# Attention and a gated MLP on one core: the last batch's normalization split over three engines, its spatial blocks in a row, its last products by token tile

## The chip, the cores and the metric

The kernel runs on one core of a Trainium2 chip. The core has a matrix engine (TensorE, PE in the profile; its weight loads are listed apart as PEld), a vector engine (VectorE, DVE), an engine for functions of one argument (ScalarE, ACT), a general engine (GpSimd, POOL) and a sync engine (SP) that here only issues DMAs. Each engine works through its own queue in order; an instruction waits for semaphores that others raise. The engines share a working memory of 128 partitions (SBUF); matmul results go to a second memory (PSUM) in buffers of 512 fp32 columns or multiples, and POOL does not touch those.

The metric is the time of one execution on the device in microseconds (us); lower is better. The times shown are medians of several executions. The profile is of one execution, which has its own time.

## The reference

Two layers, each for 8 batches of 384 tokens:

```python
# attention: 16 query heads, 4 key/value heads, head size 64
scores = scale * np.matmul(q, k.transpose(0, 1, 3, 2))
attn = softmax(scores);  x = np.matmul(attn, v)          # x: (8, 384, 1024) once the heads are joined
# gated MLP with a spatial (token to token) product
h = np.maximum(x @ w_in, 0.0)                            # w_in: 1024 x 1024
u, v = h[..., :512], h[..., 512:]
v_n = (v - mu) / np.sqrt(var + 1e-06)                    # mean and variance over the 512 features
v_s = np.einsum('ts,bsd->btd', w_spatial, v_n) + b_spatial[None, :, None]
out = (u * v_s) @ w_out                                  # w_out: 512 x 1024, out: (8, 384, 1024) fp32
```

The output is fp32; the kernel's matmuls take fp16 and accumulate in fp32.

## The kernel before

The 384 tokens of a batch are three tiles of 128 (`NT = 3`). The 1024 inner features of x are eight blocks (`NB = 8`), the 512 features of u and of v four blocks (`NM = 4`).

The program's order is written out by hand. The main loop (L594 on) goes over 18 score steps per batch: two score matmuls, an exponential on ACT, then the weighting with v. Between these it takes work of the MLP from a generator, `stream()` (L424), so many matmul columns per step (`run_fill`). The MLP of a batch runs behind its own attention, under the attention of the next one. For batch 7, the last, there is no next one: what is left of its MLP when the main loop has ended is issued in one go (`for _ in fill`). Each engine gets its instructions in the order in which this generator and the loop issue them, and runs them in that order.

What `stream()` does for a batch:

- `v_tile(b, st)` (L288): v of one token tile, eight matmuls of 128x512 (L294); then on DVE a relu into SBUF (`vr`, L304) and the statistics (L306, L307).
- `u_block(b, m)` (L358): u of one feature block for all tokens, transposed, so features on partitions and 384 tokens as columns: eight matmuls of 128x384 (L361), then a relu on ACT into `uT` (L372). In block 0, after the fourth matmul, `normal(b)` is issued.
- `normal(b)` (L311): the reciprocal standard deviation on ACT (L314, L315), minus mean times that on DVE (`nmr`, L316), and for each of the three token tiles the normalized `vn` as one multiply-add on POOL (L322), 128x512 to fp16.
- `gate(b, m)` (L375): one spatial block. Three matmuls of 128x384 over the three tiles of `vn` (L380) into `psp`; DVE adds the bias (`g`, L390); then the product with `uT` into `gT` (L392). That product is on POOL, in the last batch on DVE for blocks 1 and 3.
- `project(b, tt, half)` (L395): the output of one token tile and one half of its columns: four matmuls over the blocks of `gT` (L406), a copy from PSUM to SBUF (L415; the first half on DVE, the second on ACT), and an output DMA from SP's queue. In the last batch each piece has its own DMA (L419), and the last half of the last tile is cut in two pieces of 256 columns.

In the last batch the order before is: v of tiles 1 and 2, u of blocks 0, 1 and 2, gates 0 and 1, u of block 3, gates 2 and 3, then the six projections. Tile 0 of v comes earlier, in front of the projections of batch 6.

PSUM buffers of `pv`, `pu`, `psp` and `po` come from one pool of three (`ps_ck`), handed out in the order of use: a matmul group that begins in a buffer waits for the reader of the group three places before it. The first spatial block takes over the buffer of u's block 0, so it waits for that block's relu. The scores have a pool of their own (`ps_sc`, two buffers).

Of the kernel before, what the change touches and what calls it, by code (L numbers as in the profile page):

```python
# [9 lines left out]
FP32 = mybir.dt.float32  # L10
FP16 = mybir.dt.float16
AF = mybir.ActivationFunctionType
ALU = mybir.AluOpType
# [4 lines left out]
def kernel(  # L18
# [16 lines left out]
    nc = tc.nc  # L35
    P = 128
    B, HQ, S, D = q.shape
# [4 lines left out]
    NT = S // P  # L42
    NB = DM // P
    NM = DH // P
    G = HQ // HKV
    assert (HQ, HKV, S, D, DM, DFF) == (16, 4, 384, 64, 1024, 1024)
    scale = D ** -0.5
# [8 lines left out]
    moe = ctx.enter_context(tc.tile_pool(name="moe", bufs=2))  # L56
    small = ctx.enter_context(tc.tile_pool(name="small", bufs=4))
    ops = ctx.enter_context(tc.tile_pool(name="ops", bufs=4))
    ps_sc = ctx.enter_context(tc.tile_pool(name="ps_sc", bufs=2, space=PSUM))
    ps_av = ctx.enter_context(tc.tile_pool(name="ps_av", bufs=1, space=PSUM))  # L60
    ps_ck = ctx.enter_context(tc.tile_pool(name="ps_ck", bufs=3, space=PSUM))
# [29 lines left out]
    def load_q0(j, lo, hi, eng):  # L91
# [9 lines left out]
    load_q0(0, 1, 3, nc.sync)  # L101
    load_q0(1, 1, 3, nc.sync)

    need = {AF.Exp, AF.Relu, AF.Copy, AF.Ln}
    set_id = next(
        i for i, (_, f) in enumerate(get_activation_tables(nc.m.arch).items()) if need <= f
    )
# [2 lines left out]
            name=nc.get_next_instruction_name(), act_func_set_id=set_id, ins=[], outs=[]  # L110
# [3 lines left out]
    w_in16 = cst.tile([P, NB, DFF], FP16, name="w_in16")  # L114
    w_out16 = cst.tile([P, NM, DM], FP16, name="w_out16")
    wsT16 = cst.tile([P, NT, S], FP16, name="wsT16")
# [27 lines left out]
    bias_b = cst.tile([P, S], FP32, name="bias_b")  # L144
# [121 lines left out]
    def x_tile(b):  # L266
        if b not in xts:
            xts[b] = att.tile([P, NT, NB, P], FP16, name=f"xt_{b}", tag="xt")
        return xts[b]
# [16 lines left out]
    mvs, v_rs, v_ns, uTs, gTs, osbs = {}, {}, {}, {}, {}, {}  # L286

    def v_tile(b, st):  # L288
        if st == 0:
            mvs[b] = small.tile([P, NT, 2], FP32, name=f"mv_{b}", tag="mv")  # L290
            v_rs[b] = []
        pv = ps_ck.tile([P, 512], FP32, name=f"pv_{b}_{st}", tag="ck")
        for kt in range(NB):
            nc.tensor.matmul(  # L294
                pv,
                x_tile(b)[:, st, kt],
                w_in16[:, kt, DH:DFF],
                start=(kt == 0),
                stop=(kt == NB - 1),
            )  # L300
            if kt < NB - 1:
                yield 512
        vr = moe.tile([P, DH], FP32, name=f"vr_{b}_{st}", tag="vr", bufs=4)
        nc.vector.tensor_scalar(vr, pv, 0.0, None, op0=ALU.max)  # L304
        stats = small.tile([P, 6], FP32, name=f"stats_{b}_{st}", tag="stats")
        nc.vector.bn_stats(stats, vr)  # L306
        nc.vector.bn_aggr(mvs[b][:, st, :], stats)  # L307
        v_rs[b].append(vr)
        yield 512

    def normal(b):  # L311
        rstd = small.tile([P, NT], FP32, name=f"rstd_{b}", tag="rstd")
        nmr = small.tile([P, NT], FP32, name=f"nmr_{b}", tag="nmr")
        nc.scalar.activation(rstd, mvs[b][:, :, 1], AF.Ln, bias=eps_t)  # L314
        nc.scalar.activation(rstd, rstd, AF.Exp, scale=-0.5)  # L315
        nc.vector.scalar_tensor_tensor(  # L316
            nmr, mvs[b][:, :, 0], -1.0, rstd, op0=ALU.mult, op1=ALU.mult
        )
        v_ns[b] = []
        for st in range(NT):  # L320
            vn = moe.tile([P, DH], FP16, name=f"vn_{b}_{st}", tag="vn", bufs=6)
            nc.gpsimd.tensor_scalar(  # L322
                vn,
                v_rs[b][st],
                rstd[:, st : st + 1],
                nmr[:, st : st + 1],
                op0=ALU.mult,
                op1=ALU.add,
            )
            v_ns[b].append(vn)  # L330

    def uT_tile(b):
        if b not in uTs:
            uTs[b] = moe.tile([P, NM, S], FP16, name=f"uT_{b}", tag="uT")
        return uTs[b]
# [22 lines left out]
    def u_block(b, m):  # L358
        pu = ps_ck.tile([P, 512], FP32, name=f"pu_{b}_{m}", tag="ck")
        for kt in range(NB):  # L360
            nc.tensor.matmul(  # L361
                pu[:, 0:S].rearrange("p (t s) -> p t s", t=NT),
                w_in16[:, kt, m * P : (m + 1) * P],
                x_tile(b)[:, :, kt],
                start=(kt == 0),
                stop=(kt == NB - 1),
            )
            if m == 0 and kt == 3:
                normal(b)
            if kt < NB - 1:  # L370
                yield S
        nc.scalar.activation(uT_tile(b)[:, m, :], pu[:, 0:S], AF.Relu)  # L372
        yield S

    def gate(b, m):  # L375
        if m == 0:
            gTs[b] = moe.tile([P, NM, S], FP16, name=f"gT_{b}", tag="gT")
        psp = ps_ck.tile([P, 512], FP32, name=f"psp_{b}_{m}", tag="ck")
        for st in range(NT):
            nc.tensor.matmul(  # L380
                psp[:, 0:S],
                v_ns[b][st][:, m * P : (m + 1) * P],
                wsT16[:, st, :],
                start=(st == 0),
                stop=(st == NT - 1),
            )
            if st < NT - 1:
                yield S
        g = moe.tile([P, S], FP32, name=f"g_{b}_{m}", tag="g", bufs=4)
        nc.vector.tensor_tensor(g, psp[:, 0:S], bias_b, ALU.add)  # L390
        by = nc.vector if b == B - 1 and m % 2 else nc.gpsimd
        by.tensor_tensor(gTs[b][:, m, :], g, uTs[b][:, m, :], ALU.mult)  # L392
        yield S

    def project(b, tt, half):  # L395
        last = b == B - 1
        rows = out[b].rearrange("(p t) d -> p t d", t=NT)
        if half == 0:
            osbs[b, tt] = ops.tile([P, DM], FP32, name=f"osb_{b}_{tt}", tag="osb")
        osb = osbs[b, tt]  # L400

        cuts = (512, 768, 1024) if last and tt == NT - 1 and half else (512 * half, 512 * half + 512)
        for i, (lo, hi) in enumerate(zip(cuts, cuts[1:])):
            po = ps_ck.tile([P, 512], FP32, name=f"po_{b}_{tt}_{half}_{i}", tag="ck")
            for m in range(NM):
                nc.tensor.matmul(  # L406
                    po[:, 0 : hi - lo],
                    gTs[b][:, m, tt * P : (tt + 1) * P],
                    w_out16[:, m, lo:hi],
                    start=(m == 0),  # L410
                    stop=(m == NM - 1),
                )
                if m < NM - 1:
                    yield hi - lo
            (nc.scalar.copy if half and not i else nc.vector.tensor_copy)(  # L415
                osb[:, lo:hi], po[:, 0 : hi - lo]
            )
            if last:
                nc.sync.dma_start(rows[:, tt, lo:hi], osb[:, lo:hi])  # L419
            elif half:  # L420
                nc.sync.dma_start(rows[:, tt, :], osb)
            yield hi - lo

    def stream():  # L424


        for b in range(B):
            last = b == B - 1
            if b == 0:
                yield from v_tile(0, 0)  # L430
                yield from v_tile(0, 1)
                yield from u_tile(0, 0)
                yield from v_tile(0, 2)
                yield from u_tile(0, 1)
                yield from u_tile(0, 2)
            else:
                yield from v_tile(b, 1)
                yield from v_tile(b, 2)
                for m in range(NM):
                    yield from u_block(b, m)  # L440
                    if last and m == 2:
                        yield from gate(b, 0)
                        yield from gate(b, 1)
            for m in range(2 if last else 0, NM):
                yield from gate(b, m)
            if not last:
                yield from v_tile(b + 1, 0)
            for tt in range(NT):
                for half in range(2):
                    yield from project(b, tt, half)  # L450
# [108 lines left out]
    for b in range(B):  # L559
# [16 lines left out]
        for m in range(6):  # L576
# [4 lines left out]
            elif m > 3:  # L581
                at(s0 + 3 * m + 5, x_turn, b, 2, 4 * (m - 4), 4 * (m - 3))

    fill = stream()
    owed = 0.0
    total = NU * B
# [7 lines left out]
    for n in range(total + 6):  # L594
# [7 lines left out]
        for hh in range(2):  # L602
            b, r = divmod(n - 3 - hh, NU)
# [42 lines left out]
```

## Time and profile before

| | |
|---|---|
| time, median of 3 runs | 253.52 us (253.1 to 254.39) |
| the profiled execution: its own time | 253.12 us |
| its span, first to last instruction | 251.3 us |
| PE busy | 240.9 us, 96% of the span, 2430 matmuls |
| ACT busy | 168.2 us, 67% |
| DVE busy | 139.7 us, 56% |
| POOL busy | 98.3 us, 39% |
| granted TensorE clock | 1.00 |
| HBM read and written | 25.95 MB and 12.58 MB |

The profile names an instruction group by its line, engine and operation, with the tiles it writes and reads (`psp<-wsT,vn`: psp written from wsT and vn), the shapes, how many there were and how long they took. "Idle before" is the time for which the engine had nothing to do ahead of such an instruction, and the arrow names what ended it. The chain of waits is followed back from the last instruction: at each step to what released it, or to the instruction ahead of it on the same engine. Matmuls are pipelined: the next starts before the one ahead has ended, so a stream of them is measured by the distance of their starts.

### The profile page before, as it was taken

How to read it: one execution, taken by the hardware profiler on the slowest of the kernel's cores; microseconds unless marked ns; L12 is line 12 of the kernel's file. 1: busy time of each engine (PE TensorE's matmuls, PEld its weight loads, DVE VectorE, ACT ScalarE, POOL GpSimd, SP SyncE). 2: the span in 40 equal slices, each digit the busy share in tenths (PEclk: the TensorE clock that was granted, in tenths of full speed). 3: DMA queues.
4: the chain of work that ended last, by engine and by line, in shares of the span. 5: the costliest groups of instructions: out<-in, count | busy, mean ns of one | idle time of the engine just before them, and what ended most of it. 6: DMA issues, size and time to landing. Idle time of an engine off the chain costs nothing.

```text
span 251.3 us, 6020 instructions
## 1 busy us (share of the span) xinstructions
PE 240.9 (96%) x2430; PEld 125.7 (50%) x2430; DVE 139.7 (56%) x368; ACT 168.2 (67%) x215; POOL 98.3 (39%) x142
## 2 busy tenths in 40 slices
PE   7898998999999999999999999999999999999883
PEld 7564657534455444544455445544455445544442
DVE  2455776854626755474626655474636655465462
ACT  3996566678696687768696687768696687741211
POOL 2698837871035701392036602391035003320320
PEclk9999999999999999999999999999999999999999
DMA  7999998999289964997399956997392452106006
GB/s 179 268 285 251 301 285 238 297 224 265 88 182 330 171 230 85 266 233 216 121 199 324 185 200 66 281 253 227 111 171 49 111 183 44 34 12 250 0 22 232
DMA packets 73981, 46.93 MB, mean 187 GB/s; under 512 B 48113, under 2 KB 68913, under 8 KB 73953
## 3 DMA queue, kind: packets, MB, share of 16 engines
q1 hardware_dynamic: 68832, 37.63, 59.4%
q0 software_dynamic: 4080, 8.65, 13.8%
q8 instruction: 19, 0.31, 0.5%
q10 hardware_dynamic: 1040, 0.26, 0.5%
q14 instruction: 10, 0.07, 0.1%
HBM read 25.95 MB, written 12.58 MB: 153 GB/s over the span
## 4 chain that ended last, share of the span: by engine, by line
PE 87%; DVE 7%; issue 1%; ACT 1%; POOL 1%; POOLq 0%; DVEq 0%
PE av L247 17%; PE pv L294 16%; PE sc L233 15%; PE po L406 15%; PE pu L361 13%; PE psp L380 6%; PE warm L504 3%; DVE stats L306 2%; DVE vr L304 2%; DVE x L259 2%; PE pu L344 1%; PE qps L200 1%; ACT aT L240 1%; POOL vn L322 1%; PE xps L275 1%
## 5 line engine op out<-in xcount | busy, mean ns | idle before, releaser
L240 ACT ACTIVATE aT<-sc 128x1024 f16<-128x1024 f32 x144 | 139.6, 1021 | 52.9 <-PE sc L233 52.7
L247 PEld LDWEIGHTS <-aT 128*128 128x128 f16 x1152 | 43.4, 97 | 32.9 <-DVE x L259 12.9
L322 POOL TENSOR_SCALAR vn<-vr,rstd,nmr 128x512 f16<-128x512 f32 x24 | 18.1, 767 | 99.6 <-DVE r L257 85.7
L247 PE MATMUL av<-v,aT 128*128 128x65 f16 x1152 | 52.3, 194 | 1.6 <-DVE x L259 1.2
L294 PE MATMUL pv<-w_in,xt 128*128 128x512 f16 x192 | 49.5, 378 | 0.0
L257 DVE RECIPROCAL r<-av 128x4 f32<-128x4 f32 x96 | 17.1, 178 | 58.3 <-PE av L247 57.8
L406 PE MATMUL po<-w_out,gT 128*128 128x512 f16 (+1 forms) x196 | 48.2, 375 | 0.9 <-POOL gT L392 0.9
L233 PE MATMUL sc<-qT,kT 64*128 64x512 f16 x288 | 45.0, 382 | 0.7 <-ACT aT L240 0.4
L259 DVE TENSOR_TENSOR x<-av,r 128x256 f16<-128x256 f32 x96 | 40.7, 424 | 3.4
L361 PE MATMUL pu<-xt,w_in 128*128 128x384 f16 x224 | 41.7, 326 | 0.0
L392 POOL TENSOR_TENSOR gT<-g,uT 128x384 f16<-128x384 f32 x30 | 26.5, 914 | 29.4 <-DVE g L390 29.4
L361 PEld LDWEIGHTS <-w_in 128*128 128x128 f16 x224 | 20.2, 97 | 14.7 <-issue 2.5
L406 PEld LDWEIGHTS <-gT 128*128 128x128 f16 x196 | 17.0, 97 | 19.4 <-issue 2.9
L170 POOL CAST q<-q 128x768 f16<-128x768 f32 (+1 forms) x36 | 24.9, 732 | 3.1 <-DMA q<-in_q_dram 3.1
L415 DVE COPY osb<-po 128x512 f32<-128x512 f32 (+1 forms) x25 | 16.8, 671 | 11.6 <-PE po L406 11.6
L294 PEld LDWEIGHTS <-xt 128*128 128x128 f16 x192 | 16.2, 97 | 13.5 <-issue 0.7
L415 ACT COPY osb<-po 128x512 f32<-128x512 f32 (+1 forms) x24 | 13.9, 580 | 12.4 <-PE po L406 12.3
L304 DVE TENSOR_SCALAR vr<-pv 128x512 f32<-128x512 f32 x24 | 16.5, 687 | 10.2 <-PE pv L294 10.0
L233 PEld LDWEIGHTS <-kT 64*128 64x128 f16 x288 | 8.9, 94 | 26.6 <-issue 24.4
L380 PE MATMUL psp<-wsT,vn 128*128 128x384 f16 x96 | 19.6, 326 | 0.6 <-POOL vn L322 0.6
L390 DVE TENSOR_TENSOR g<-psp,bias_b 128x384 f32<-128x384 f32 x32 | 16.4, 552 | 5.9 <-PE psp L380 5.9
L306 DVE BATCH_NORM_STATS2 stats<-vr 128x6 f32<-128x512 f32 x24 | 16.7, 695 | 0.8
(49 smaller groups left out, 125.8 us busy)
## 6 DMA issues: line engine op xcount, KB each, us to landing
out_dram<-osb SPq DMA_DIRECT2D x21, 512.0 KB, 2.9
q<-in_q_dram SPq DMA_DIRECT2D x10, 768.0 KB, 7.2
q<-in_q_dram POOLq DMA_DIRECT2D x4, 768.0 KB, 10.4
v<-in_v_dram SPq DMA_DIRECT2D x6, 384.0 KB, 8.7
w_in<-in_moe_w_in_dram POOLq DMA_DIRECT2D x4, 512.0 KB, 9.7
k<-in_k_dram SPq DMA_DIRECT2D x5, 384.0 KB, 4.2
out_dram<-osb SPq DMA_DIRECT2D x5, 256.0 KB, 2.0
q<-in_q_dram SPq DMA_DIRECT2D x2, 512.0 KB, 7.2
```

The costliest lines, as they stand in the source:

```text
L170: f(q16s[b, j][:, lo:hi, :, hh, :], src[:, hh, lo:hi])
L233: nc.tensor.matmul(sc[:, hh], kTs[b][half, j, t * P : (t + 1) * P], qTs[b, j][half, qt], start=True, stop=True,)
L240: nc.scalar.activation(aTs[b, m][:, t], sc, AF.Exp, scale=scale)
L247: nc.tensor.matmul(av[:, i, :], aTs[b, m][:, t, hh, i * P : (i + 1) * P], v1[b % 2][:, 2 * j + hh, t, 0 : D + 1], start=(t == 0), stop=(t ...
L259: nc.vector.tensor_tensor(x16s[b][:, qt, blk : blk + 2].rearrange("p k (i d) -> p (k i) d", i=2), av[:, :, 0:D], r.to_broadcast([P, G, D]) ...
L294: nc.tensor.matmul(pv, x_tile(b)[:, st, kt], w_in16[:, kt, DH:DFF], start=(kt == 0), stop=(kt == NB - 1),)
L306: nc.vector.bn_stats(stats, vr)
L361: nc.tensor.matmul(pu[:, 0:S].rearrange("p (t s) -> p t s", t=NT), w_in16[:, kt, m * P : (m + 1) * P], x_tile(b)[:, :, kt], start=(kt == 0 ...
L380: nc.tensor.matmul(psp[:, 0:S], v_ns[b][st][:, m * P : (m + 1) * P], wsT16[:, st, :], start=(st == 0), stop=(st == NT - 1),)
L392: by.tensor_tensor(gTs[b][:, m, :], g, uTs[b][:, m, :], ALU.mult)
L406: nc.tensor.matmul(po[:, 0 : hi - lo], gTs[b][:, m, tt * P : (tt + 1) * P], w_out16[:, m, lo:hi], start=(m == 0), stop=(m == NM - 1),)
L415: (nc.scalar.copy if half and not i else nc.vector.tensor_copy)(osb[:, lo:hi], po[:, 0 : hi - lo])
```

## The change

Three places, all of them for the last batch alone; the lines of the other batches are renumbered but the same.

1. `normal(b)`: of the three normalized tiles, tile 0 stays on POOL, tile 1 is computed on DVE and tile 2 on ACT, there as an activation with the function Identity, a scale and a bias per partition. Identity joins the list of functions from which the table set is chosen at the start.
2. `stream()`: u of blocks 0, 1 and 2, then a new function `last_gate()`. It runs the four spatial blocks one after another, then u of block 3 in two pieces: the first token tile (128 columns) and the other two (256 columns), in PSUM buffers of the scores' pool, each with its own relu on ACT. The products of blocks 0 and 1 are on POOL, over all tokens. Those of blocks 2 and 3 are cut as block 3 is: block 2's first token tile on POOL, the other three pieces on DVE.
3. `project()`: the last half of the last token tile is cut at 896 instead of 768, into 384 and 128 columns.

```diff
-    need = {AF.Exp, AF.Relu, AF.Copy, AF.Ln}
+    need = {AF.Exp, AF.Relu, AF.Copy, AF.Ln, AF.Identity}
...
-            nc.gpsimd.tensor_scalar(
-                vn,
-                v_rs[b][st],
-                rstd[:, st : st + 1],
-                nmr[:, st : st + 1],
-                op0=ALU.mult,
-                op1=ALU.add,
-            )
+            a, c = rstd[:, st : st + 1], nmr[:, st : st + 1]
+            if b == B - 1 and st == 2:
+                nc.scalar.activation(vn, v_rs[b][st], AF.Identity, scale=a, bias=c)
+            else:
+                by = nc.vector if b == B - 1 and st == 1 else nc.gpsimd
+                by.tensor_scalar(vn, v_rs[b][st], a, c, op0=ALU.mult, op1=ALU.add)
...
-        by = nc.vector if b == B - 1 and m % 2 else nc.gpsimd
-        by.tensor_tensor(gTs[b][:, m, :], g, uTs[b][:, m, :], ALU.mult)
+        nc.gpsimd.tensor_tensor(gTs[b][:, m, :], g, uTs[b][:, m, :], ALU.mult)
         yield S
+
+    def last_gate():
+        b = B - 1
+        gT = gTs[b] = moe.tile([P, NM, S], FP16, name=f"gT_{b}", tag="gT")
+        uT = uT_tile(b)
+        gs = []
+        for m in range(NM):
+            psp = ps_ck.tile([P, 512], FP32, name=f"psp_{b}_{m}", tag="ck")
+            for st in range(NT):
+                nc.tensor.matmul(
+                    psp[:, 0:S],
+                    v_ns[b][st][:, m * P : (m + 1) * P],
+                    wsT16[:, st, :],
+                    start=(st == 0),
+                    stop=(st == NT - 1),
+                )
+                yield S
+            g = moe.tile([P, S], FP32, name=f"g_{b}_{m}", tag="g", bufs=4)
+            nc.vector.tensor_tensor(g, psp[:, 0:S], bias_b, ALU.add)
+            gs.append(g)
+            if m < 2:
+                nc.gpsimd.tensor_tensor(gT[:, m], g, uT[:, m], ALU.mult)
+        first, rest = slice(0, P), slice(P, S)
+        m = NM - 1
+        for part in (first, rest):
+            pu = ps_sc.tile([P, 512], FP32, name=f"pu_{b}_{m}_{part.start}", tag="sc")
+            n = part.stop - part.start
+            for kt in range(NB):
+                nc.tensor.matmul(
+                    pu[:, 0:n].rearrange("p (t s) -> p t s", s=P),
+                    w_in16[:, kt, m * P : (m + 1) * P],
+                    x_tile(b)[:, part.start // P : part.stop // P, kt],
+                    start=(kt == 0),
+                    stop=(kt == NB - 1),
+                )
+                yield n
+            nc.scalar.activation(uT[:, m, part], pu[:, 0:n], AF.Relu)
+        for by, m, part in (
+            (nc.gpsimd, 2, first),
+            (nc.vector, 3, first),
+            (nc.vector, 2, rest),
+            (nc.vector, 3, rest),
+        ):
+            by.tensor_tensor(gT[:, m, part], gs[m][:, part], uT[:, m, part], ALU.mult)
...
-        cuts = (512, 768, 1024) if last and tt == NT - 1 and half else (512 * half, 512 * half + 512)
+        cuts = (512, 896, 1024) if last and tt == NT - 1 and half else (512 * half, 512 * half + 512)
...
-                for m in range(NM):
-                    yield from u_block(b, m)
-                    if last and m == 2:
-                        yield from gate(b, 0)
-                        yield from gate(b, 1)
-            for m in range(2 if last else 0, NM):
-                yield from gate(b, m)
+                for m in range(NM - last):
+                    yield from u_block(b, m)
+            if last:
+                yield from last_gate()
+            else:
+                for m in range(NM):
+                    yield from gate(b, m)
```

## The prediction

> **What bounds the kernel now.** I read the chain of waits on the page first, then the timeline of the last stretch on all engines, then the line of the gate product, then the output queue.
>
> ```profile
> PE 87%; DVE 7%; issue 1%; ACT 1%; POOL 1%; POOLq 0%; DVEq 0%
> ```
>
> TensorE (PE) sets 87% of the span. With one batch after another something always fills it, so what the other engines do counts only where PE has nothing else to run. That is the last batch: from 229.3 us on there is no attention work left, and the edit touches nothing before it. Timeline of the last batch (start, duration in us, engine, line, operation, count, idle before):
>
> ```profile
> 235.04 0.20 ACT L315 ACTIVATE rstd<-rstd 128x3 f32<-128x3 f32 x1
> 235.15 0.91 ACT L372 ACTIVATE uT<-pu 128x384 f16<-128x384 f32 x2
> 235.28 0.16 DVE L316 SCALAR_TENSOR_TENSOR nmr<-mv,rstd 128x3 f32<-128x3 f32 x1 [0.60 <-ACT rstd L315]
> 235.64 2.26 POOL L322 TENSOR_SCALAR vn<-vr,rstd,nmr 128x512 f16<-128x512 f32 x3 [13.84 <-PE pu L361]
> 236.67 0.33 PE L380 MATMUL psp<-wsT,vn 128*128 128x384 f16 x1
> 237.21 0.34 PE L380 MATMUL psp<-wsT,vn 128*128 128x384 f16 x1 [0.22 <-POOL vn L322]
> 237.96 0.82 PE L380 MATMUL psp<-wsT,vn 128*128 128x384 f16 x4 [0.41 <-POOL vn L322]
> ```
>
> The first spatial block needs the three normalized tiles in turn, and GpSimd (POOL) delivers them 0.75 us apart. PE takes a 128x384 matmul every 0.1625 us: four in 0.82 us are three steps and one matmul of 0.326. The third should have started at 236.67 + 2 x 0.1625 = 236.995 and started at 237.96: **0.97 us lost**. (The idle figures in brackets are smaller, because the modelled ends of matmuls reach into the gaps; starts are the safer measure.)
>
> ```profile
> 238.41 1.04 DVE L390 TENSOR_TENSOR g<-psp,bias_b 128x384 f32<-128x384 f32 x2 [2.97 <-PE psp L380]
> 238.62 1.46 PE L361 MATMUL pu<-xt,w_in 128*128 128x384 f16 x8
> 239.11 0.91 POOL L392 TENSOR_TENSOR gT<-g,uT 128x384 f16<-128x384 f32 x1 [1.21 <-DVE g L390]
> 239.56 0.89 DVE L392 TENSOR_TENSOR gT<-g,uT 128x384 f16<-128x384 f32 x1
> 240.68 1.04 DVE L390 TENSOR_TENSOR g<-psp,bias_b 128x384 f32<-128x384 f32 x2 [0.24 <-PE psp L380]
> 240.90 0.59 PE L406 MATMUL po<-w_out,gT 128*128 128x512 f16 x2
> 241.38 0.91 POOL L392 TENSOR_TENSOR gT<-g,uT 128x384 f16<-128x384 f32 x1 [1.36 <-DVE g L390]
> 241.83 0.88 DVE L392 TENSOR_TENSOR gT<-g,uT 128x384 f16<-128x384 f32 x1
> 242.35 5.13 PE L406 MATMUL po<-w_out,gT 128*128 128x512 f16 x26 [0.86 <-POOL gT L392]
> ```
>
> The first projection runs two matmuls, 0.216 us apart (0.59 - 0.379 for the second's own length), and then waits: the products of blocks 2 and 3 come after the last spatial block. The third should start at 240.90 + 0.43 = 241.33 and starts at 242.35, 1.02 late; the fourth starts at 242.76 (the next weight load in the timeline), 0.20 later than a step would give. **1.22 us lost**; both stalls make 2.19.
>
> The two DVE rows of L392 hold a second fact. Each began while POOL's product was running and ended 0.42 us after POOL's end (240.45 against 240.02, 242.71 against 242.29), so 0.42 is its own cost and 0.46 waiting. The g rows (L390), which read one operand from PSUM, keep their usual 0.55 beside POOL.
>
> ```profile
> 243.91 4.76 SPq L419 DMA_DIRECT2D out_dram<-osb  x7
> 247.52 0.42 DVE L415 COPY osb<-po 128x256 f32<-128x256 f32 x1 [0.18 <-PE po L406]
> ```
>
> The seventh output DMA is issued until 243.91 + 4.76 = 248.67; that issue takes 0.40 us, so it starts at 248.26, 0.32 after its copy has ended at 247.94. The tail is paced by SP's queue, which takes a DMA every 0.43 to 0.47 us there, not by the last copy.
>
> **Part 1, normalizing on three engines.** Removed: two of POOL's three instructions (1.50 us of the chain). POOL keeps vn_0, ready at 236.41 as now. DVE takes vn_1 behind L316, from 235.47. No row shows this operation on DVE; the nearest are the cast 128x256 f16 from f32 in SBUF (0.29, half the size) and the statistics over 128x512 f32 (0.70). Either way it is ready by 236.2; PE wants it at about 236.9. ACT takes vn_2 ahead of the four relus. Bounds: 0.58 (copy of 128x512, L415) and 0.204 (L315, three elements) + 2 x 0.093 (what the pointer operand adds, L314's 0.297 less L315) + 512 x 0.00083 (L240's 1021 ns at 1024 elements against L372's 489 at 384) = 0.815. I take 0.80, since this instruction has two pointer operands: 235.48 to 236.28. What is queued behind it is the relu of u's block 0, and the first spatial block waits for that relu, because it takes over the PSUM buffer of pu_0. It starts at 236.20 (neighbours on ACT overlap by some 0.08), takes 0.49, and PE goes on 0.05 later, at 236.74 instead of 236.67. So 0.90 of the 0.97 is won; with ACT at its bounds 0.97 or 0.88.
>
> **Part 2, spatial blocks in a row, u's block 3 by token tile, products by token tile.** In the built order PE runs the 12 spatial matmuls, then 8 of 128x128, 8 of 128x256, then the projections. The steps are 0.1625; 0.057 (four transposes of 128x128 in 0.39 us, the last 0.219 long); 0.109 (nine matmuls in 1.25 us, one of 512 and eight of 256). From 236.74: 1.95 + 0.45 + 0.87, so the first projection could start at 240.01. Block 3 costs 1.32 instead of 8 x 0.1625 = 1.30: **+0.02**. The new PSUM tiles lie in the pool of the scores, unused by then. When are the products there?
> - g of block 0 starts 0.44 after the third spatial matmul (as 238.41 after 237.96): 237.51, ends 238.07. POOL's gT0 starts 0.15 later and takes 0.91: 239.13. gT1 follows 0.87 after its start (the pace of POOL's products in other batches): 240.00, wanted at 240.23.
> - gT2 of the first token tile, 128x128 on POOL, has no row. A third of 0.914 is 0.30; 0.914 less 256 elements at the casts' 0.82 ns is 0.70. I take 0.40, near the first, as the fixed part of POOL's casts is small (826 ns at 768, 405 at 256). 239.96 to 240.36; wanted at 240.44, so it is just in time; at 0.70 it costs 0.27. I put down 0.05.
> - gT3 of the first tile: its relu ends about 239.6 (0.27, below the 0.37 of a 128x256 copy), DVE waits for POOL's gT1 until 240.0 and needs some 0.15: wanted at 240.66.
> - The rest of gT2 and gT3, 128x256 on DVE, 0.28 to 0.42 each, end by 241.3; wanted in the second token tile, after eight matmuls, at about 242.2. This cover of 0.9 us hides them and the late first eviction on DVE.
>
> So of the 1.22 us, **1.17** is won.
>
> **Part 3, 384 and 128 columns.** 4 x 0.1625 + 4 x 0.057 = 0.88 against 8 x 0.109 = 0.87. After the last full projection's copy, SP issues three DMAs in both versions. The 384-column copy on ACT (0.48, between 0.37 and 0.58) lets SP go within 0.02 us of now, and the small DVE copy is done before SP is free. The last DMA carries 64 KB instead of 128, the one before it 192: between -0.1 and +0.1, taken as **0**.
>
> **Sum** against the profiled execution (253.12 us, span 251.3): -0.90 - 1.17 + 0.02 = -2.05, so 251.07. The median shown is 0.40 above that execution: 251.47, say **251.5**.
>
> **Rivals.**
> *A, DVE and POOL block each other at both places (14%).* The L392 rows show that one waits out the other. If vn_1 gets ahead of vn_0, POOL starts at 235.76 to 236.17 and vn_0 is ready at 236.53 to 236.94, so the first spatial matmul slips by up to 0.25 beyond the 236.74 above. If gT3's first part goes before gT2's, that one ends at about 240.6, another 0.2. Gain 1.6, time 251.9. For it: two rows out of two. Against: all of DVE's earlier waits had a POOL instruction already running, and no row shows a tensor-scalar of DVE doing this.
> The Trainium skill, "SBUF — State Buffer", section "Who interferes with whom", says that DVE and GpSimd share one pair of SBUF ports as an exclusive lock. The holders it names are a DVE instruction with two SBUF inputs (against a GpSimd one that reads SBUF) and a copy or tensor-scalar in a two-port mode. The trace agrees for the first kind (0.42 after POOL's end, twice); for the second no run here shows it; if vn_1 runs in that mode, this rival's first half is certain by that rule.
>
> *B, one of the two stalls stays (11%)*, most likely at the first projection, if POOL's short product costs 0.7 and the waits of A come on top. Gain 0.9 to 1.2, time 252.4. For it: three products still pass one slow engine one after another. Against: they start 0.9 us earlier than now.
>
> *C, slower: ACT changes its function table for the new function and back (5%).* The table load at the start takes 1.28 us (the row of L108). Two of them ahead of the relus put the relu of block 0 at 239.3, so the first spatial block starts 2.6 us late while 2.2 are saved: 253.9. It decides from the second load on; with one the kernel would still gain 0.8. Against: the changed program, as built, holds one table load, as now.
>
> *D, the end is set by output DMAs in any case (4%)*: 253.5. Against: the first of the seven waits for the first projection's copy, so all of them move with PE.
>
> **Chances and range.** The forecast has 66%. Half a percent, 1.27 us, is about what a measurement of this kernel can tell from no change; forecast and A lie beyond it, B and D mostly within, C on the other side. Faster 0.80, within 0.13, slower 0.07. The range: 2.19 us and 0.1 of the tail won in full from a median like the lowest run (253.1) gives 250.8; the upper end includes A and B: **250.7 to 252.8**.
>
> **What would show it.** Twelve spatial matmuls 0.16 apart from about 236.75 (part 1); no idle time on PE from there to the last projection, which then starts near 240.0 (part 2); the last DMA's issue 2.0 us after the start of the last 512-column matmul, as now: 248.26 against 246.23 (part 3). A vn_0 that ends after 236.5 speaks for A, a gap among the first four projection matmuls for B, a second table load for C. I am wrong if PE runs on without gaps and the time still does not fall, or if a gap opens between the spatial blocks, where I have PE waiting for nothing.

## The result and the profile after

| | before | after |
|---|---|---|
| time, median | 253.54 us (252.98 to 256.42) | 251.55 us (251.06 to 252.43) |
| ratio, 95% interval | | 0.9919 [0.9894, 0.9945] |
| the profiled execution / its span | 253.12 / 251.3 us | 251.51 / 249.7 us |

The change saves 1.99 us, 0.8%; the prediction was 251.5.

Single executions differ before the change acts. The start of the last matmul of v (L294, `pv`) is a common mark: nothing ahead of it was edited but the list of ACT's functions. It lies at 232.55 us before and 232.94 after. So I measure from this mark. "T0" is the start of the last 512-column projection matmul.

| from the mark, us | before | after | won |
|---|---|---|---|
| first spatial matmul | 4.116 | 4.225 | -0.11 |
| third spatial matmul, after the first | 1.294 | 0.324 | 0.97 |
| third spatial matmul to T0 | 8.263 | 7.096 | 1.17 |
| T0, from the mark | 13.673 | 11.645 | **2.03** |
| T0 to the end of the span | 5.12 | 5.12 | 0 |

The chain of waits on the page of after has 91% on PE, where it had 87%:

```profile
PE 91%; DVE 6%; ACT 1%; issue 1%; POOL 0%; POOLq 0%
```

Followed through the last batch (start, duration, what) it stays on PE from v to the last projection:

```profile
233.97 3.25 PE pu L359 x20
237.22 2.06 PE psp L402 x12
239.27 1.32 PE pu L421 x16
240.59 5.25 PE po L449 x28
245.85 0.02 issue
245.87 0.29 DVE osb L458
```

The timeline of after has the same stretch on all engines (start, duration, engine, line, operation, count, idle before):

```profile
235.66 0.16 DVE L316 SCALAR_TENSOR_TENSOR nmr<-mv,rstd 128x3 f32<-128x3 f32 x1 [0.60 <-ACT rstd L315]
235.86 0.55 DVE L327 TENSOR_SCALAR vn<-vr,rstd,nmr 128x512 f16<-128x512 f32 x1
235.92 0.81 ACT L324 ACTIVATE vn<-vr,nmr,rstd 128x512 f16<-128x512 f32 x1 [0.29 <-DVE nmr L316]
236.03 1.02 POOL L327 TENSOR_SCALAR vn<-vr,rstd,nmr 128x512 f16<-128x512 f32 x1 [13.85 <-PE pu L359]
236.64 1.23 ACT L370 ACTIVATE uT<-pu 128x384 f16<-128x384 f32 x3
237.10 1.78 PEld L402 LDWEIGHTS <-vn 128*128 128x128 f16 x12 [0.27 <-POOL vn L327]
237.16 2.11 PE L402 MATMUL psp<-wsT,vn 128*128 128x384 f16 x12
...
239.11 1.48 PE L421 MATMUL pu<-xt,w_in 128*128 128x128 f16 x16
...
240.07 1.40 DVE L436 TENSOR_TENSOR gT<-g,uT 128x128 f16<-128x128 f32 x3
240.37 0.48 POOL L436 TENSOR_TENSOR gT<-g,uT 128x128 f16<-128x128 f32 x1
240.43 5.40 PE L449 MATMUL po<-w_out,gT 128*128 128x512 f16 x28
```

Four things are to be seen. The twelve spatial matmuls are one group of 2.11 us: eleven steps of 0.1625 and one matmul of 0.326. The 28 projection matmuls are one group; the third among them came 0.04 us later than a step, the fourth 0.01. And POOL's normalization, 0.75 us a tile before, took 1.02, because DVE had begun its own 0.17 earlier. The first spatial matmul comes 0.27 after the start of the last matmul of u (0.16 in the kernel before), which is a step of 0.16 and 0.11 of waiting.

### The profile page after: what moved, and what is told of

Its sections match the earlier page's. It is cut to its first block, busy times and chain, and to the rows that moved or that the text cites. A ratio compares the mean times of both kernels' runs of the same rounds, so it can differ in the third digit from the quotient of the medians.

```text
span 249.7 us, 6038 instructions
## 1 busy us (share of the span) xinstructions
PE 240.9 (96%) x2438; PEld 126.2 (51%) x2438; DVE 139.9 (56%) x370; ACT 169.1 (68%) x217; POOL 97.4 (39%) x141
## 4 chain that ended last, share of the span: by engine, by line
PE 91%; DVE 6%; ACT 1%; issue 1%; POOL 0%; POOLq 0%
PE av L247 17%; PE pv L294 16%; PE sc L233 15%; PE po L449 15%; PE pu L359 14%; PE psp L378 6%; PE warm L547 3%; DVE x L259 2%; DVE stats L306 1%; DVE vr L304 1%; PE pu L342 1%; PE qps L200 1%; ACT aT L240 1%; PE psp L402 1%; PE xps L275 1%
## 5 line engine op out<-in xcount | busy, mean ns | idle before, releaser
L327 POOL TENSOR_SCALAR vn<-vr,rstd,nmr 128x512 f16<-128x512 f32 x22 | 16.9, 778 | 100.0 <-DVE r L257 86.2
L294 PE MATMUL pv<-w_in,xt 128*128 128x512 f16 x192 | 49.6, 379 | 0.0
L449 PE MATMUL po<-w_out,gT 128*128 128x512 f16 (+2 forms) x196 | 47.9, 375 | 0.0
L359 PE MATMUL pu<-xt,w_in 128*128 128x384 f16 x216 | 40.2, 326 | 0.0
L389 POOL TENSOR_TENSOR gT<-g,uT 128x384 f16<-128x384 f32 x28 | 24.7, 914 | 26.8 <-DVE g L388 26.8
L359 PEld LDWEIGHTS <-w_in 128*128 128x128 f16 x216 | 19.4, 98 | 14.2 <-issue 2.5
L294 PEld LDWEIGHTS <-xt 128*128 128x128 f16 x192 | 16.1, 97 | 13.5 <-issue 0.6
L378 PE MATMUL psp<-wsT,vn 128*128 128x384 f16 x84 | 17.0, 327 | 0.0
L388 DVE TENSOR_TENSOR g<-psp,bias_b 128x384 f32<-128x384 f32 x28 | 14.4, 552 | 2.7 <-PE psp L378 2.7
```

Source lines behind the costliest of these rows:

```text
L294: nc.tensor.matmul(pv, x_tile(b)[:, st, kt], w_in16[:, kt, DH:DFF], start=(kt == 0), stop=(kt == NB - 1),)
L359: nc.tensor.matmul(pu[:, 0:S].rearrange("p (t s) -> p t s", t=NT), w_in16[:, kt, m * P : (m + 1) * P], x_tile(b)[:, :, kt], start=(kt == 0 ...
L378: nc.tensor.matmul(psp[:, 0:S], v_ns[b][st][:, m * P : (m + 1) * P], wsT16[:, st, :], start=(st == 0), stop=(st == NT - 1),)
L389: nc.gpsimd.tensor_tensor(gTs[b][:, m, :], g, uTs[b][:, m, :], ALU.mult)
L449: nc.tensor.matmul(po[:, 0 : hi - lo], gTs[b][:, m, tt * P : (tt + 1) * P], w_out16[:, m, lo:hi], start=(m == 0), stop=(m == NM - 1),)
```

## The experiments

**Which part brings what.** Each part was built into the kernel before by itself. Theory: the two stalls are separate and their gains add up; rival: one gain needs the other. First the normalization (e1), with everything else as before:

```diff
...
-            nc.gpsimd.tensor_scalar(
...
+            if b == B - 1 and st == 2:
+                nc.scalar.activation(vn, v_rs[b][st], AF.Identity, scale=a, bias=c)
+            else:
+                by = nc.vector if b == B - 1 and st == 1 else nc.gpsimd
+                by.tensor_scalar(vn, v_rs[b][st], a, c, op0=ALU.mult, op1=ALU.add)
```

> Only the normalization is spread over the three engines; blocks, products and cuts are as before. Theory (two separate stalls of TensorE, each with its own cause): the third spatial matmul follows the first by 0.33 us instead of 1.29, everything behind it moves up by 0.86, and the wait of 1.2 us at the first projection stays. Time 0.86 us below the kernel before. Rival (one bound, the products on GpSimd and VectorE): TensorE only gets to the projection earlier and waits there longer, about 2.1 us; time within 0.2 us of the kernel before.

Measured: 252.55 us (252.37 to 252.91) against 253.52; ratio 0.9962 [0.9948, 0.9977], 0.97 us. Then `last_gate()` with POOL normalizing all three tiles and the cut at 768 (e2); against the changed kernel:

```diff
...
-            if b == B - 1 and st == 2:
-                nc.scalar.activation(vn, v_rs[b][st], AF.Identity, scale=a, bias=c)
-            else:
-                by = nc.vector if b == B - 1 and st == 1 else nc.gpsimd
...
+            nc.gpsimd.tensor_scalar(
...
-        cuts = (512, 896, 1024) if last and tt == NT - 1 and half else (512 * half, 512 * half + 512)
+        cuts = (512, 768, 1024) if last and tt == NT - 1 and half else (512 * half, 512 * half + 512)
```

> Only the spatial blocks in a row, block 3 of u and the products by token tile; normalization on GpSimd alone and the last half in 256 and 256 columns, as before. Theory (separate stalls): the 0.97 us among the first spatial matmuls stay, the wait at the first projection falls from 1.2 to under 0.1; time 1.15 us below the kernel before. Rival (the parts need each other: with vn_2 late, the products start as late as before and the wait at the projection comes back): gain under 0.5 us.

Measured: 252.42; ratio 0.9956 [0.9942, 0.997], 1.10 us. Timeline of e1, then of e2:

```profile
237.42 1.14 PE L378 MATMUL psp<-wsT,vn 128*128 128x384 f16 x6
...
240.67 0.59 PE L404 MATMUL po<-w_out,gT 128*128 128x512 f16 x2
242.12 1.24 PE L404 MATMUL po<-w_out,gT 128*128 128x512 f16 x4 [0.86 <-POOL gT L390]
```

```profile
236.93 0.33 PE L404 MATMUL psp<-wsT,vn 128*128 128x384 f16 x1
237.48 0.34 PE L404 MATMUL psp<-wsT,vn 128*128 128x384 f16 x1 [0.22 <-POOL vn L322]
238.22 1.80 PE L404 MATMUL psp<-wsT,vn 128*128 128x384 f16 x10 [0.41 <-POOL vn L322]
...
241.18 2.15 PE L451 MATMUL po<-w_out,gT 128*128 128x512 f16 x9
```

e1 runs its first six spatial matmuls without a gap and keeps the wait for POOL's product in front of the third projection matmul; e2 has it the other way round. Each part removes its own stall and leaves the other's at its old size. From the mark to T0, e1 wins 0.87 us and e2 1.16 in their traces, which add up to the 2.03 of the change. Last the cut by itself (e3), in the kernel before:

```diff
-        cuts = (512, 768, 1024) if last and tt == NT - 1 and half else (512 * half, 512 * half + 512)
+        cuts = (512, 896, 1024) if last and tt == NT - 1 and half else (512 * half, 512 * half + 512)
```

> Only the cut of the last half, 384 and 128 columns instead of 256 and 256. Theory (the tail is paced by the queue that issues the output DMAs): no change, within 0.15 us; the last DMA is issued 2.03 us after the start of the last 512-column matmul, as before. Rival (the last copy paces the tail): the copy is 0.13 us shorter and the time falls by as much or more.

Measured: 253.5 against 253.52; ratio 0.9999 [0.9987, 1.0012]. The last copy takes 0.29 instead of 0.42 us, and the last DMA is issued at T0 + 2.04 as before. The three differences add up to 2.09; the change as a whole gave 1.99, and 1.77 and 1.88 when it was measured twice more, each time beside other kernels (e8 beside e6 and e7, e11 beside e9 and e10). Both are a little below the 1.9 to 2.1 expected, and within their intervals:

> The changed kernel itself, beside the others on the same chip, as their measure: 1.9 to 2.1 us below the kernel before.

251.68 (251.02 to 251.74), ratio 0.9922 [0.9909, 0.9936].

> The changed kernel once more as the measure on this chip: 1.9 to 2.1 us below the kernel before.

251.56 (251.25 to 253.01), ratio 0.9936 [0.9914, 0.9959].

**What the 0.11 us ahead of the first spatial matmul is.** The profile names POOL's `vn` as releaser, which DVE had delayed. But the relu of u's block 0 on ACT, queued behind `vn_2`, ended at 237.11, 0.06 after POOL's tile at 237.05. From here on the edits are against the changed kernel. e4 lets POOL begin first, by a statistics instruction on DVE that nobody reads:

```diff
+                if by is nc.vector:
+                    again = small.tile([P, 6], FP32, name="stats_again", tag="again", bufs=1)
+                    nc.vector.bn_stats(again, v_rs[b][2])
                 by.tensor_scalar(vn, v_rs[b][st], a, c, op0=ALU.mult, op1=ALU.add)
```

> The changed kernel with one more VectorE instruction (the statistics of the last tile of v a second time, into a tile that nobody reads, 0.70 us) ahead of VectorE's normalization, which then starts while GpSimd's is half done. Theory (one of the two waits out the other, whoever started first): GpSimd's normalization takes 0.77 us again instead of 1.02; VectorE's is issued 0.7 us later, stands until GpSimd's has ended and ends about 0.3 us after that. Rival (they share the memory's bandwidth): GpSimd's stays near 1.0 us, since the two still overlap, and VectorE's keeps its 0.55.

```profile
236.04 0.77 POOL L330 TENSOR_SCALAR vn<-vr,rstd,nmr 128x512 f16<-128x512 f32 x1 [13.84 <-PE pu L362]
236.35 0.73 DVE L330 TENSOR_SCALAR vn<-vr,rstd,nmr 128x512 f16<-128x512 f32 x1
236.65 1.23 ACT L373 ACTIVATE uT<-pu 128x384 f16<-128x384 f32 x3
237.17 2.11 PE L405 MATMUL psp<-wsT,vn 128*128 128x384 f16 x12
```

POOL's tile is back at 0.77 and ready at 236.81; now DVE is the one that waits (0.73 instead of 0.55, ending 0.28 after POOL). Yet the first spatial matmul starts 4.220 after the mark, against 4.225. What it follows, by 0.05, is the first relu, which ends at 237.12. So freeing POOL wins nothing by itself. (One execution, 251.48.) e5 takes the relu out from behind `vn_2`:

```diff
-                nc.scalar.activation(vn, v_rs[b][st], AF.Identity, scale=a, bias=c)
+                later.append((vn, v_rs[b][st], a, c))
...
         nc.scalar.activation(uT_tile(b)[:, m, :], pu[:, 0:S], AF.Relu)
+        for vn, vr, a, c in later:
+            nc.scalar.activation(vn, vr, AF.Identity, scale=a, bias=c)
+        later.clear()
```

> The changed kernel, but on ScalarE the relu of block 0 of u goes ahead of the normalization of tile 2 (it has its input long before). Theory (that relu, queued behind 0.81 us of normalization, is what holds the first spatial matmul 0.11 us after the last matmul of u): the relu ends 1.1 us earlier and the distance from the start of the last u matmul to the first spatial one falls from 0.27 us to at most 0.22; what is left then is GpSimd's tile, held up by VectorE. Rival (GpSimd's tile alone, which the profile names): the distance stays at 0.27.

```profile
235.33 0.47 ACT L372 ACTIVATE uT<-pu 128x384 f16<-128x384 f32 x1
235.82 1.02 POOL L327 TENSOR_SCALAR vn<-vr,rstd,nmr 128x512 f16<-128x512 f32 x1 [13.85 <-PE pu L361]
236.89 1.31 PE L407 MATMUL psp<-wsT,vn 128*128 128x384 f16 x7
```

The relu is done at 235.80, the wait shrinks from 0.27 to 0.215, and POOL's delayed tile, ready at 236.84, is now what ends it. (One execution, 251.22.) The 0.11 was two limits close behind each other: about 0.055 is the relu's alone, and the other 0.055 is only won if POOL's tile comes earlier as well.

**What paces the tail.** The prediction blamed SP's queue. e6 gives the 384-column DMA to ACT's queue:

```diff
-                nc.sync.dma_start(rows[:, tt, lo:hi], osb[:, lo:hi])
+                by = nc.scalar if len(cuts) > 2 and not i else nc.sync
+                by.dma_start(rows[:, tt, lo:hi], osb[:, lo:hi])
```

> The changed kernel, but the output DMA of the 384 columns is issued from ScalarE's queue instead of SP's. Theory (the tail is paced by SP's queue, 0.43 to 0.47 us a DMA): the 128-column DMA is issued right after its copy, about 0.4 us earlier, and the time falls by 0.2 to 0.4 us against the changed kernel. Rival (the tail is paced by the transfers themselves, which share the 16 DMA engines): the issues move and the landings do not; no change.

Measured: 251.56; ratio 0.992 [0.9906, 0.9935], as after. The last DMA is issued at T0 + 1.61 instead of 2.03, so the edit did its work; the last landing (counted when SP's queue sees it) is at T0 + 3.93 instead of 3.92. The end is at 5.20 instead of 5.12, because SP's queue checks one semaphore more behind that landing, 0.06 us. The step on SP's queue falls. The busy share of the DMA engines shows why (tenths, slices of 0.125 us from 245 us on; after, then e6):

```profile
DMA  9999689898304999999999993000000000000000
```

```profile
DMA  9986799994039989999999940000000000000000
```

After the short hole the last three transfers (256, 192 and 64 KB) fill about 1.6 us of 9s with no hole between them, in both kernels. The earlier issue of the last one did not end the tail earlier: its 64 KB landed 0.44 earlier, and the 192 KB, issued when they were before, landed 0.18 later. e7 joins e5 and e6, and also gives tile 0 to DVE and tile 1 to POOL, so that the delayed tile is wanted later:

```diff
...
-                by = nc.vector if b == B - 1 and st == 1 else nc.gpsimd
+                by = nc.vector if b == B - 1 and st == 0 else nc.gpsimd
...
```

> e5 and e6 together, and tile 0 of the normalized v on VectorE, tile 1 on GpSimd, so that the tile that is held up is wanted one matmul later. Theory: the first spatial matmul follows the last matmul of u by one step (0.16 us), 0.11 us less than in the changed kernel; with the tail 0.3 to 0.5 us below the changed kernel. Rival for the first part: the second spatial matmul now waits for tile 1, and the 0.11 us come back there.

Measured: 251.5 (251.06 to 252.99); ratio 0.9927 [0.9906, 0.9949]. In the trace the 0.11 is gone: the first spatial matmul comes 4.116 after the mark, one step behind the last of u, and T0 at 11.539 instead of 11.645. The end comes 16.73 after the mark instead of 16.77. In the times, where 0.3 to 0.5 us were expected, this can't be told from after.

If the first of the last three transfers sets the rest, it has to be issued earlier. e9 cuts its copy in two, so that ACT and DVE do half each:

```diff
+            if last and tt == NT - 1 and not half:
+                nc.scalar.copy(osb[:, 0:256], po[:, 0:256])
+                nc.vector.tensor_copy(osb[:, 256:512], po[:, 256:512])
...
```

> The changed kernel, but the copy of the last 512-column half from PSUM is shared: 256 columns on ScalarE, 256 on VectorE, so that its output DMA is issued about 0.26 us earlier (0.88 instead of 1.14 us after the start of the last 512-column matmul). Theory (after e6: the queue of issues and the transfers both end the tail, one as late as the other): the first of the last three DMAs lands earlier, but the last one is still issued 2.03 us after that matmul, lands 3.9 us after it, and the time stays within 0.1 us of the changed kernel. Rival (the transfers alone): the time falls by about 0.26 us.

```profile
245.16 0.42 DVE L460 COPY osb<-po 128x256 f32<-128x256 f32 x1 [1.44 <-ACT osb L459]
```

DVE's half waited for ACT's: the two read one PSUM buffer, and the program as built puts them one after the other. So the edit made the issue later, T0 + 1.27 instead of 1.14, and the last landing went with it, T0 + 4.06 instead of 3.92. (251.59; ratio 0.9928 [0.9915, 0.9941].) e10 is e7 with the same two copies:

> e7 with the shared copy of e9: now the issues and the transfers both move. Theory (both ends of the tail moved): the last two DMAs are issued about 1.6 us after the start of the last 512-column matmul and the last landing comes 0.25 to 0.4 us earlier than in the changed kernel (3.9 us after that matmul there); time 0.35 to 0.5 us below the changed kernel with the 0.1 us at the spatial blocks. Rival (a DMA's own time from issue to landing, 2.2 to 2.35 us for 192 KB, whatever runs beside it): the landing stays at 3.9 us and only the 0.1 us is gained.

251.81; ratio 0.9938 [0.992, 0.9955]. The last two DMAs were issued at T0 + 1.57 and 1.69, where e9 issued them at 1.70 and 2.18, and the last landing stayed at T0 + 4.06. e12 computes the two halves as two matmul groups in two PSUM buffers, so that ACT copies the first half while PE works on the second; one DMA takes both. The rest is e7:

```diff
...
-        cuts = (512, 896, 1024) if last and tt == NT - 1 and half else (512 * half, 512 * half + 512)
+        cuts = (512 * half, 512 * half + 512)
+        if last and tt == NT - 1:
+            cuts = (512, 896, 1024) if half else (0, 256, 512)
...
+            if last and len(cuts) > 2 and not half:
+                if i:
+                    nc.sync.dma_start(rows[:, tt, 0:512], osb[:, 0:512])
...
```

> e7, with the first half of the last token tile as two matmul groups of 256 columns in two PSUM buffers, copied by ScalarE and VectorE side by side (in e9 and e10 the second copy of one buffer waited for the first), and one output DMA for both. It is issued about 0.76 us after the start of the last matmul of those groups, 0.25 us earlier against TensorE's work than in e7. Theory (the last three transfers follow one another from the first issue on; in e6, e7, e9, e10 and the changed kernel the last landing came 2.78 to 2.80 us after that first issue, whatever the other two did): the landing comes 2.8 us after the first issue, the span ends about 0.25 us earlier than e7's against the last u matmul, time about 0.35 us below the changed kernel. Rival (each DMA's own time from issue to landing): the other two are issued no earlier than in e7, and the end stays.

```profile
245.26 0.33 SPq L470 DMA_DIRECT2D out_dram<-osb  x1
245.93 0.38 ACTq L473 DMA_DIRECT2D out_dram<-osb  x1
245.96 0.33 SPq L473 DMA_DIRECT2D out_dram<-osb  x1
```

Measured: 251.25 (251.14 to 251.47); ratio 0.9915 [0.9899, 0.9931]. All six kernels side by side, from the mark:

| us | after | e6 | e7 | e9 | e10 | e12 |
|---|---|---|---|---|---|---|
| issue of the first of the last three DMAs | 12.78 | 12.78 | 12.68 | 12.91 | 12.81 | 12.45 |
| last landing | 15.56 | 15.57 | 15.48 | 15.70 | 15.59 | 15.30 |
| difference | 2.78 | 2.79 | 2.80 | 2.79 | 2.78 | 2.85 |

The difference holds within 0.07 us, whichever queue issued the later two and however early. The rival of e12 was that each DMA takes its own time from issue to landing. Against it, e12 issued the later two no earlier than e7 (13.12 and 13.16 after the mark, against 13.11 and 13.15), and the last landing still came 0.18 earlier.

The landings also follow the bytes. Behind that of the 256 KB, the 128 and 128 KB of before landed after another 0.35 and 0.35 us, the 192 and 64 KB of the changed kernel after another 0.55 and 0.17, though the issues were equally far apart in both (0.43 and 0.47).

The end of the span is 16.57 after the mark in e12, 0.20 before after's and 0.16 before e7's, where 0.25 was expected. Its median is the lowest of all that were run several times, but its interval overlaps with those of the change; that it beats the change is seen in the trace and not settled by the times.

## Why the prediction was right, and where it was not

*Part 1, 0.90 predicted, 0.86 measured.* The mechanism was the one given: the relu of block 0 behind `vn_2` delays the first spatial matmul. I had it 0.07 late, it was 0.11: `vn_2` took 0.815, the upper bound, not 0.80, and began 0.06 later on the clock of the mark than put down, while the relu took 0.47 instead of 0.49. e4 and e5 show the relu as the later of two limits; without it POOL's tile would still have cost about half of the 0.11. DVE's tile took 0.55 (bounds 0.29 and 0.70).

*"POOL keeps vn_0, ready at 236.41 as now" was wrong.* It was ready at 237.05, which is 236.66 on the clock of before. This is the first half of rival A. DVE follows its own `nmr` after 0.04 us and POOL needs 0.20, so DVE got ahead, and POOL's instruction took 1.017 instead of about 0.77. It cost nothing only because the relu was later still, by 0.06 us, which was luck.
The Trainium skill, "SBUF — State Buffer", section "Who interferes with whom", says that a tensor-scalar of DVE in a two-port mode blocks GpSimd, and that the order of issue decides who is blocked. The trace of before had no such pair. These traces agree: with DVE first POOL takes 1.017, with POOL first (e4) POOL takes 0.77 and DVE 0.73 instead of 0.55. In which mode DVE ran, no trace here shows.

*Part 2, 1.17 predicted, 1.17 measured.* From the first spatial to the first projection matmul I had 240.01 - 236.74 = 3.27 us, and it is 3.27. The second half of rival A happened too. The single pieces of the products, by line and engine (ns minimum/median/maximum, first and last start):

```profile
L436 DVE TENSOR_TENSOR gT<-g,uT x3: 421/492/645, 240.1 to 241.0; 128x256 f16<-128x256 f32 x2, 128x128 f16<-128x128 f32 x1
...
L436 POOL TENSOR_TENSOR gT<-g,uT x1: 478/478/478, 240.4 to 240.4; 128x128 f16<-128x128 f32 x1
```

DVE's first piece (0.492) waited for POOL's gT1 until 240.41; POOL's short product, which began at 240.37, then waited for that piece until 240.56 and ended 0.29 later. So its 0.478 (I took 0.40) holds 0.19 of waiting and an own cost near the lower bound of 0.30. It cost PE 0.04 and 0.01, where I had put down 0.05: the sum is right, but by two errors that cancel, an own cost taken too high and a wait left out. Rival A was therefore right about what happens and wrong about the price, 0.4 us, since each blocked piece had almost as much time to spare as it lost. The 0.42 us that I read from the rows of L392 as the own cost of DVE's product of 128x384 was too low: in after, one of 128x256 takes 0.421 with POOL idle. The 0.42 is only what is left of it behind POOL's end.

*Part 3, 0 predicted, 0 measured (e3), for a reason that did not hold.* "The tail is paced by SP's queue" is the step that failed. e6 took 0.42 us off that queue and won nothing. The queue's pace of 0.43 to 0.47 us was real, but the transfers behind it are as slow: 512 KB in 1.6 us. The runs put in its place: the last landing follows the first of the last three issues by 2.8 us, so what counts is the copy in front of that issue. That the bytes set the 2.8 us fits the unbroken 9s and the landings, which follow the sizes; no run changed the sum of the bytes.

*Rivals B, C and D.* B: the gaps left at the projections are 0.05 us. C: there is no second table load ahead of the relus. D: the tail moved with PE, 5.12 us after T0 in both.

*The sum.* 2.05 predicted, 2.03 in the trace. The times say 1.99, 1.77 and 1.88. The 0.40 us added for the median happened to be about what the mark differs by (0.39); executions vary by 0.67 us ahead of it (232.53 to 233.20 over the 14 profiles), so neither is more than chance.

## What to carry to other kernels

Where one engine paces a stall, count what an instruction displaces in the queue that takes it over: here the 0.11 us given back came from a relu behind the moved tile, not from the tile, and a tile held up by another engine stood only 0.06 us in front of it. The releaser that a profile names may be one of two within 0.1 us; only moving one shows what the other costs. For a tail of output DMAs, look at the busy share of the DMA engines first. Here it had no hole: an earlier first issue moved the end, a second queue and a smaller last piece did not. Fewer bytes were not tried.

## What the runs showed of the hardware that was not expected

- A DVE product that has waited out POOL needs less time behind POOL's end than it takes by itself. The one of 128x256 took 0.421 us with POOL idle, and ended 0.28 after POOL's end where it had been waiting; the 128x128 one ended 0.146 after, the two of 128x384 in the kernel before 0.41. That is about 1.05 ns a column and next to no fixed part. Either the fixed part passes during the wait, or POOL lets go before its recorded end; no run here tells the two apart.
- Two copies on two engines out of one PSUM buffer did not overlap (e9): DVE's waited for ACT's, by a semaphore of the built program. Whether the chip would let them overlap was not tried.
- POOL's multiply-add of 128x512 ended 0.64 us after DVE's. It had stood for 0.38 by then, and of its 0.77 alone only about 0.13 was saved.
